# Where the gate products of a batch stand among its token tiles, and how many filler matmuls TensorE gets

## The chip, the cores and the metric

The kernel runs on one core of a Trainium2 chip. The core has TensorE (PE in the profile; its weight loads are PEld), VectorE (DVE), ScalarE (ACT), GpSimd (POOL), and SyncE (SP), which issues most of the transfers. The engines run in parallel. Each takes its own instructions in order and waits on semaphores for the others. TensorE's clock has two levels, 1.2 and 2.4 GHz, and the profile gives the granted clock as a share of the higher one. The metric is the device time of one execution, in microseconds (us), lower being better.

## What is computed

Linear attention without a mask, a norm per head, and then a mixture of eight experts of which each token uses one:

```python
kv = np.einsum('bhsd,bhse->bhde', k, v)          # 8 batches, 8 heads, 576 tokens, 64 wide
out = np.einsum('bhsd,bhde->bhse', q, kv)
out = out / np.sqrt(np.mean(out * out, -1) + 1e-6) * g_norm
x = out                                          # 4608 tokens x 512
logits = x @ w_gate;  e_idx = argmax(logits);  gate_w = softmax(logits)[e_idx]
eom = sigmoid(x @ w_output_gate)
y = gate_w * eom[e_idx] * (relu(x @ w1[e_idx]) @ w2[e_idx])   # 512 -> 1024 -> 512
```

## The kernel before

There are two stages. The first makes all tokens' attention rows and decides each token's expert. It writes the rows to a table `xs` in device memory. The second stage gathers the rows of one expert after another and runs the two large products (`mm1`, `mm2`). The change touches the first stage only.

**The first stage** goes over the 8 batches in `p1_main`. A batch has 576 tokens, which is 4.5 tiles of 128. For batch b, PE does this:

- `kv_part(b)`: 40 products of a head's k with its v, into the PSUM tile `kvps`, over five slices s of the tokens. I call it kv(b). ScalarE copies the result into `augs[b % 3]`, and VectorE copies it into `kvc`.
- `kvT_part`: two transposes of `kvc` into `kvTps`. ScalarE copies them out as `kvT`.
- `m_part(b)`: 8 small products of `kvT` with the gate weights into `mps`. ScalarE copies them into the gate columns of the same `augs` tile. These are the gate products of the title, and I call the step m(b).
- `run_out`: one token tile (`out_tile(g)`, here T0 to T35). It is 8 products of the query with `augs`, into `ops`. The same products give attention rows and gate sums, so a tile of batch b needs m(b). ScalarE empties `ops` with three instructions (`xrow`, `sq`, `gp`).

The tiles that run during batch b are those that batch b-1 completed, so they trail by one batch. In batches 1 to 7 they are T0-3, T4-8, T9-12, T13-17, T18-21, T22-26 and T27-30. T31 to T35 follow after the last batch. `ops` and `mps` share two PSUM buffers (`ps_b`), and `kvps`, `kvTps` and `cps` share two others (`ps_t`).

**Fillers.** `constant` multiplies a tile of ones by itself into a part of PSUM that nobody reads. Its only purpose is to give TensorE something to do. `COLD` holds the numbers: 2 in front of each of the first four slices in the first three batches, 20 more at the start, 2 ahead of `kvT`, 3 ahead of m, and 3 of twice the width behind m in a tile `cps` of their own.

**Routing.** The tiles form four groups: T0-7, T8-15, T16-23 and T24-35. Each has a chain of small VectorE instructions (`route`), which `run_out` moves on by a piece per tile. A chain needs PE twice. `rps` gives positions (after T14, T22 and T27 for the first three groups), and `tblps` fills the table (in front of T17, in front of T26 and behind T30). For each tile of the group `tblps` needs a `la` tile; the first two groups have theirs made on GpSimd, eight in a row, once VectorE has made `rlon`. In VectorE's queue the copy `kvc` of the same batch stands ahead of those pieces. When the third group is placed, its tail (`xtail`) is written to `xs` and the first expert's rows are gathered. From there on the second stage begins.

**Transfers.** SP issues all loads (`ld`: slices `kvm` of keys and values, remainders `rem`, queries `qT`) in the order of `loads`, then the writes of `xrow` and `xtail`, then the weights (`wraw`). PE, ACT, DVE and POOL run in the order of the program text; SP's order is set by a scheduler.

Of the kernel before, what the change touches and what calls it, by code (L numbers as in the profile page):

```python
# [11 lines left out]
F32 = mybir.dt.float32  # L12
# [9 lines left out]
P = 128  # L22
B, H, S, D = 8, 8, 576, 64
# [60 lines left out]


COLD_B = 3
COLD = (2, 20, 2, 3, 3)

ROUND = 1.5 * 2.0 ** 30

# [49 lines left out]
def body(ctx: ExitStack, tc: tile.TileContext, kvm, rem, qT, wg, gn, w1, w2, kc, xs, tab, out):  # L140
    nc = tc.nc
# [27 lines left out]
    ps_t = main.enter_context(tc.tile_pool(name="ps_t", bufs=2, space=psum))  # L169
# [266 lines left out]
    ones = c1.tile([P, P], BF16, name="ones")  # L436
# [45 lines left out]
    def constant(ps, n, start=True):  # L482

        for _ in range(n):
            k = ps.shape[1] // P
            nc.tensor.matmul(ps, ones, ones.unsqueeze(1).to_broadcast([P, k, P]), start=start, stop=start)

    def kv_part(b):

# [3 lines left out]
        for s in range(5):  # L493
            if s < 4 and b < COLD_B:
                constant(ps[:, 256:512], COLD[0] + (COLD[1] if b == 0 and s == 0 else 0), s == 0)
            for p in range(NP):
# [18 lines left out]
    def kvT_part(cp):  # L515

        ps = ps_t.tile([P, 512], F32, name="kvTps", tag="t")
        constant(ps[:, 256:512], COLD[2])
        ps = ps[:, 0:256].rearrange("q (i x) -> q i x", i=2)
        for i in range(2):  # L520
            nc.tensor.transpose(ps[:, i, :], cp[:, i * P:(i + 1) * P], ident)
        t = wk.tile([P, 2, P], F32, name="kvT", bufs=1)
        nc.scalar.copy(t, ps)
        return t

    def m_part(b, kvT):
        a = augs[b % 3]
        ps = ps_b.tile([P, 2, 512], F32, name="mps", tag="big")
        constant(ps[:, 1, 256:512], COLD[3])
        for i in range(2):  # L530
# [61 lines left out]
    def sums():  # L592

        sq, o, gi = squares.pop(0)
        nc.vector.tensor_reduce(out=o, in_=sq, axis=AX.X, op=ALU.add)  # L595
        if gi is not None:
            routing.append(route(gi))
# [212 lines left out]
    def open_rows(late):  # L810
        opened[late] = True
        for w in [w for w in xwrites if (w[0] >= LEAD_TILES) == late]:
            xwrites.remove(w)
            xwrite(*w)

    done_tiles = 0
# [13 lines left out]
    def run_out(limit):  # L830
        nonlocal done_tiles
        if done_tiles < limit:
            out_tile(done_tiles)
            done_tiles += 1
            if len(squares) > 1:
                sums()
            advance()
            load(SPARE)
            if not loads and not opened[0]:
                open_rows(0)  # L840
            if lead_placed and opened[0] and (0, 1, 0) not in raw and (1, 0) not in wgt:
                for c in range(1):
                    wload(0, 1, c)
            for step in HOOKS.get(done_tiles, ""):
                act(step)
# [24 lines left out]
    def p1_main():  # L870
        load(SPARE)
        for b in range(B):
            lim = tiles_ready(b - 1) if b else 0
            cp = kv_part(b)
            load(SPARE)
            run_out(lim)
            kvT = kvT_part(cp)
            run_out(lim)
            run_out(lim)
            m_part(b, kvT)  # L880
            constant(ps_t.tile([P, 512], F32, name="cps", tag="t"), COLD[4])
            while done_tiles < lim:
                run_out(lim)
        while done_tiles < NT:
            run_out(NT)
        for step in TAIL:
            act(step)
        while routing:
            advance()
# [218 lines left out]
    with ExitStack() as p3:  # L1108
# [4 lines left out]
        with tc.For_i(0, nreg) as i:  # L1113
# [19 lines left out]
            for w in (w1, w2):  # L1133
                for c in range(4):
                    t = wo.tile([P, 1024], F32, name=f"ow{len(ws)}")
# [6 lines left out]
            ps = pt.tile([P, 4, P], F32, name="ops")  # L1142
# [68 lines left out]
```

## Time and profile before

| | us |
|---|---|
| median of 3 runs | 588.94 (587.86 to 590.38) |
| the profiled execution's own time | 591.15 |
| its span, first to last instruction | 589.4 |
| PE busy in the span | 562.4 (95%) |

All times below are from the start of the span of the profiled execution. A timeline row has the start, the length, the engine, the source line, the operation, what it writes and reads, and a count; equal neighbours are merged into one row. The length of the last matmul of a row runs over into the next row, so what a step costs on PE is read from start to start. A bracket at the end of a row gives the idle time ahead of it and what ended it.

### The profile page before, as it was taken

What the parts mean: (1) busy time and instruction counts of PE and PEld (TensorE: products, weight loads), DVE (VectorE), ACT (ScalarE), POOL (GpSimd) and SP (SyncE); (2) the same over time, 40 slices, a digit from 0 to 9 for tenths busy, and PEclk for the clock granted to TensorE, in tenths of its full rate; (3) what the DMA queues carried; (4) which work ended last, traced back from release to release, by engine and by line L of the source; (5) the groups of instructions that cost most, each with busy time, mean ns of one, the idle gap of its engine ahead of it and who ended that gap; (6) DMA issues with size and microseconds to landing.
All of it is one profiled execution on the core that took longest, in us unless ns stands there. A gap on an engine that the chain in (4) does not pass through costs nothing.

```text
span 589.4 us, 10666 instructions
## 1 busy us (share of the span) xinstructions
PE 562.4 (95%) x4287; PEld 491.6 (83%) x4287; DVE 258.3 (44%) x562; ACT 223.2 (38%) x411; POOL 145.8 (25%) x150
## 2 busy tenths in 40 slices
PE   7999898869999999999999999999999999999995
PEld 4677777758798998889889987998799889889974
DVE  2136677698325556325531443244334424523410
ACT  1356555643235334323432343235234323532410
POOL 2002330401722511620172027003600540011011
PEclk9899898578999999999999999999999999999998
DMA  8999995681564622342335233524342343200001
GB/s 277 382 408 405 408 374 173 225 295 32 156 254 135 213 78 92 107 159 85 123 95 185 80 108 99 175 72 132 101 153 100 111 165 103 80 36 20 1 19 45
DMA packets 33460, 92.26 MB, mean 157 GB/s; under 512 B 8801, under 2 KB 8929, under 8 KB 33408
## 3 DMA queue, kind: packets, MB, share of 16 engines
q1 hardware_dynamic: 26672, 71.63, 34.5%
q0 software_dynamic: 6304, 19.70, 10.6%
q8 instruction: 35, 0.57, 0.4%
q10 hardware_dynamic: 432, 0.21, 0.1%
q14 instruction: 17, 0.14, 0.1%
HBM read 72.34 MB, written 19.70 MB: 156 GB/s over the span
## 4 chain that ended last, share of the span: by engine, by line
PE 79%; DMA 7%; issue 5%; DVE 4%; POOL 2%; ACT 1%; POOLq 0%; SPq 0%; DVEq 0%
PE hps L322 35%; PE yps L371 33%; PE yps L365 3%; PE tps L284 3%; DMA ld<-qT 2%; PE ops L574 2%; DMA ld<-rem 2%; PE kvps L504 2%; POOL la L752 2%; DMA ld<-kvm 2%; DMA xg<-xs,gidx 1%; DVE ss L595 1%; DMA out<-y,oidx 0%; DVE wlo L222 0%; DVE wlo L229 0%
## 5 line engine op out<-in xcount | busy, mean ns | idle before, releaser
L322 PE MATMUL hps<-xT,whi 128*128 128x256 f32 (+8 forms) x1024 | 192.7, 306 | 5.1 <-DVE hT L338 4.6
L371 PE MATMUL yps<-whi,hT 128*128 128x512 f32 (+3 forms) x592 | 195.0, 398 | 0.0
L322 PEld LDWEIGHTS hps<-xT,whi 128*128 128x128 f32 x1024 | 160.1, 191 | 7.2 <-DVE hT L338 4.2
L371 PEld LDWEIGHTS yps<-whi,hT 128*128 128x128 f32 (+3 forms) x592 | 110.1, 186 | 24.1
L322 PE MATMUL hps<-xT,wlo 128*128 128x304 f32 (+8 forms) x512 | 119.6, 305 | 0.0
L371 PE MATMUL yps<-wlo,hT 128*128 128x512 f32 (+3 forms) x296 | 115.9, 392 | 0.0
L338 DVE SCALAR_TENSOR_TENSOR hT<-hps,hT 128x512 fp32r<-128x512 f32 (+6 forms) x112 | 57.9, 518 | 124.3 <-ACT hT L337 124.3
L337 ACT ACTIVATE hT<-hps 128x512 fp32r<-128x512 f32 (+6 forms) x112 | 51.5, 460 | 144.8 <-PE hps L322 115.0
L322 PEld LDWEIGHTS hps<-xT,wlo 128*128 128x128 f32 x512 | 87.4, 191 | 0.0
L244 POOL DMA_INDIRECT xg<-xs,gidx x42 | 42.7, 1018 | 169.3 <-PE tps L284 91.8
L382 POOL DMA_INDIRECT out<-y,oidx x42 | 44.5, 1059 | 147.9 <-ACT y L381 106.6
L371 PEld LDWEIGHTS yps<-wlo,hT 128*128 128x128 f32 (+3 forms) x296 | 55.1, 186 | 11.2
L222 DVE SCALAR_TENSOR_TENSOR wlo<-wraw,gcol,whi 128x1024 fp32r<-128x1024 f32 x32 | 44.4, 1387 | 40.2 <-ACT whi L219 40.2
L381 ACT ACTIVATE y<-yps,tl 128x512 f32<-128x512 f32 (+3 forms) x37 | 25.5, 688 | 71.4 <-PE yps L371 67.6
L260 POOL TENSOR_TENSOR xg<-xg 128x512 f32<-128x512 f32 (+7 forms) x39 | 41.7, 1072 | 41.0 <-DMA xg<-xs,gidx 33.9
L289 ACT CAST xT<-tps 128x512 fp32r<-128x512 f32 (+9 forms) x45 | 23.2, 518 | 68.7 <-PE tps L284 67.1
L290 DVE TENSOR_TENSOR xT<-tps,xT 128x512 fp32r<-128x512 f32 (+9 forms) x45 | 27.1, 604 | 44.5 <-ACT xT L289 44.0
L229 DVE TENSOR_TENSOR wlo<-wraw,whi 128x1024 fp32r<-128x1024 f32 x32 | 39.2, 1224 | 14.2 <-ACT whi L226 7.1
L574 PE MATMUL ops<-aug,ld 64*128 64x80 f32 (+1 forms) x640 | 41.8, 289 | 0.6 <-issue 0.6
L574 PEld LDWEIGHTS ops<-aug,ld 64*128 64x128 f32 (+1 forms) x640 | 37.3, 194 | 5.8 <-ACT aug L536 3.0
L219 ACT ACTIVATE whi<-wraw,gcol 128x1024 fp32r<-128x1024 f32 x31 | 35.5, 1145 | 0.0
L226 ACT CAST whi<-wraw 128x1024 fp32r<-128x1024 f32 x32 | 33.3, 1041 | 1.7 <-DMA wraw<-w 1.7
(163 smaller groups left out, 400.6 us busy)
## 6 DMA issues: line engine op xcount, KB each, us to landing
wraw<-w SPq DMA_DIRECT2D x64, 512.0 KB, 3.6
ld<-kvm SPq DMA_DIRECT2D x32, 512.0 KB, 10.1
ld<-qT SPq DMA_DIRECT2D x18, 512.0 KB, 10.2
xs<-xrow SPq DMA_DIRECT2D x13, 512.0 KB, 11.6
xs<-xrow SPq DMA_DIRECT2D x2, 1280.0 KB, 15.0
ld<-rem SPq DMA_DIRECT2D x3, 512.0 KB, 10.2
xg<-xs,gidx POOLq DMA_INDIRECT x42, 3.6
out<-y,oidx POOLq DMA_INDIRECT x42, 3.1
```

Source lines behind the costliest of these rows:

```text
L219: he.activation(hi, r, AF.Copy, scale=gcol[:, 0:1])
L222: eng.scalar_tensor_tensor(out=lo, in0=r, scalar=gcol[:, 0:1], in1=hi.bitcast(F32), op0=ALU.mult, op1=ALU.subtract)
L226: he.copy(hi, r)
L229: eng.tensor_tensor(out=lo, in0=r, in1=hi.bitcast(F32), op=ALU.subtract)
L244: gathered = nc.gpsimd.indirect_dma_start(out=x[:M, :], out_offset=None, in_=rows, in_offset=bass.IndirectOffsetOnAxis(ap=gidx[:M, p, t:t ...
L260: eng.tensor_tensor(out=v, in0=v, in1=f, op=ALU.mult)
L322: nc.tensor.matmul(ps[:, j, :n], w[:, o:o + P], x[d][:, j * N:j * N + n], start=(d == 0 and k == 0), stop=(d == 3 and k == 2))
L337: nc.scalar.activation(hh, x, AF.Relu)
L338: nc.vector.scalar_tensor_tensor(out=v(h[:, l:l + n]), in0=x, scalar=0.0, in1=hh.bitcast(F32), op0=ALU.max, op1=ALU.subtract)
L371: nc.tensor.matmul(ps[:M], a, b, start=(f == 0 and k == 0), stop=(f == 7 and k == 2))
L382: i_ = nc.gpsimd.indirect_dma_start(out=out, out_offset=bass.IndirectOffsetOnAxis(ap=oidx[:M, p, t:t + 1], axis=0), in_=y[:M], in_offset=N ...
L574: nc.tensor.matmul(ps[r0:r0 + m, u, p * W:(p + 1) * W], qt[g // 2][r, p, q0:q0 + m], augs[b % 3][r, p, :], start=True, stop=True)
```

## The change

It does four things. In every batch but the last, a second tile goes ahead of `kvT`, and all the remaining tiles go between `kvT` and m, where two stood before (none is left behind m). In the last batch one tile stands there and two come behind m. The fillers are now 1 ahead of `kvT`, 1 ahead of m, and none behind m; those in kv(0) to kv(2) stay. `constant` repeats 64 columns of ones instead of 128, to the same total width. The new helper `cold` is not called.

```diff
-COLD = (2, 20, 2, 3, 3)
+COLD = (2, 20, 1, 1)
...
-            k = ps.shape[1] // P
-            nc.tensor.matmul(ps, ones, ones.unsqueeze(1).to_broadcast([P, k, P]), start=start, stop=start)
+            k = ps.shape[1] // D
+            nc.tensor.matmul(ps, ones, ones[:, 0:D].unsqueeze(1).to_broadcast([P, k, D]), start=start, stop=start)
+
+    def cold():
+        return ps_t.tile([P, 512], F32, name="cps", tag="t")
...
             run_out(lim)
+            if b + 1 < B:
+                run_out(lim)
             kvT = kvT_part(cp)
-            run_out(lim)
-            run_out(lim)
+
+            while done_tiles < (lim if b + 1 < B else lim - 2):
+                run_out(lim)
             m_part(b, kvT)
-            constant(ps_t.tile([P, 512], F32, name="cps", tag="t"), COLD[4])
             while done_tiles < lim:
                 run_out(lim)
```

**PE, batch 3**, a batch of four tiles and no routing on PE. Before, from the two tiles behind `kvT` to kv(4):

```order
L574 MATMUL ops<-aug_117,ld 128x80 x16
L486 LDWEIGHTS ones
L486 MATMUL mps<-ones 128x256
...
L534 MATMUL mps<-gw,kvT 64x16 x8
L486 LDWEIGHTS ones
L486 MATMUL cps<-ones 128x512
...
L574 MATMUL ops<-aug_117,ld 128x80 x8
L504 MATMUL kvps<-ld 64x64 x40
```

The whole of that batch behind kv(3) now:

```order
L577 MATMUL ops<-aug_117,ld 128x80 x16
L486 LDWEIGHTS ones
L486 MATMUL kvTps<-ones 128x256
L524 MATMUL kvTps<-ident,kvc 128x128 x2
L577 MATMUL ops<-aug_117,ld 128x80 x16
L486 LDWEIGHTS ones
L486 MATMUL mps<-ones 128x256
L537 MATMUL mps<-gw,kvT 64x16 x8
L507 MATMUL kvps<-ld 64x64 x40
```

The tile behind m has gone ahead of `kvT` (8 products are one tile), and m now stands directly in front of kv(4).

**PE, batch 4**, where the first group's `tblps` stands. Before, from m(4) to kv(5):

```order
L534 MATMUL mps<-gw,kvT 64x16 x8
L486 LDWEIGHTS ones
L486 MATMUL cps<-ones 128x512
...
L574 MATMUL ops<-aug_115,ld 128x80 x8
L782 LDWEIGHTS la
L782 MATMUL tblps<-rrc,la 128x96
...
L574 MATMUL ops<-aug_115,ld 128x80 x8
L504 MATMUL kvps<-ld 64x64 x40
```

Now, from the two tiles behind `kvT` to kv(5):

```order
L577 MATMUL ops<-aug_115,ld 128x80 x16
L785 LDWEIGHTS la
L785 MATMUL tblps<-rrc,la 128x96
...
L577 MATMUL ops<-aug_115,ld 128x80 x8
L486 LDWEIGHTS ones
L486 MATMUL mps<-ones 128x256
L537 MATMUL mps<-gw,kvT 64x16 x8
L507 MATMUL kvps<-ld 64x64 x40
```

The gate products m(4) and the fillers stood in front of `tblps`; m(4) with its one filler now stands behind it and behind T17. Batch 6 has the same move around T26. VectorE's order does not change at all, and ScalarE's follows PE's.

**SP, at the end of the first stage.** Before:

```order
L804 DMA xs<-xrow 128x2x512 x4
L804 DMA xs<-xtail 128x8x16
L190 TENSOR_LOAD epos
L190 ISA x2
L199 ISA
L199 DMA wraw<-w 128x1024
L804 DMA xs<-xtail 128x8x16
```

Now:

```order
L807 DMA xs<-xrow 128x2x512 x4
L807 DMA xs<-xtail 128x8x16 x2
L190 TENSOR_LOAD epos
L190 ISA x2
L199 ISA
L199 DMA wraw<-w 128x1024
```

The third group's tail has gone in front of the first weight tile's load.

## Rows read from the trace of the kernel before

**Rows 1.** Busy time of each engine from 150 us to the end of the span: length, then busy us of PE, PEld, DVE, ACT and POOL with instruction counts, then granted clock, share of the 16 DMA engines, GB/s.

```profile
150.00:589.40 439.40, 433.07 (x2545) 385.36 (x2544) 166.65 (x286) 151.19 (x240) 117.13 (x112) 1.00 0.33 109
```

**Rows 2.** PE's timeline from the end of kv(2) to kv(4).

```profile
33.70 0.62 PE L504 MATMUL kvps<-ld 64*64 64x64 f32 x14 [0.59 <-DMA ld<-rem]
...
41.73 2.70 PE L504 MATMUL kvps<-ld 128*64 128x64 f32 x80
...
49.03 0.49 PE L486 MATMUL mps<-ones 128*128 128x256 bf16 x3 [0.48 <-ACT gp L582]
49.44 0.42 PE L534 MATMUL mps<-gw,kvT 64*64 64x16 f32 x16
49.80 0.82 PE L486 MATMUL cps<-ones 128*128 128x512 bf16 x3
50.55 1.12 PE L574 MATMUL ops<-aug,ld 64*128 64x80 f32 x16
51.60 2.63 PE L504 MATMUL kvps<-ld 128*64 128x64 f32 x77
```

**Rows 3.** ScalarE's timeline, batches 2 and 3.

```profile
35.01 0.58 ACT L579 COPY xrow<-ops 128x512 f32<-128x512 f32 x1 [0.22 <-PE ops L574]
...
47.13 0.46 ACT L523 COPY kvT<-kvTps 128x256 f32<-128x256 f32 x1
47.60 0.58 ACT L579 COPY xrow<-ops 128x512 f32<-128x512 f32 x1
...
48.74 0.67 ACT L579 COPY xrow<-ops 128x512 f32<-128x512 f32 x1
...
49.93 0.30 ACT L536 COPY aug<-mps 128x64 f32<-128x64 f32 x1
```

**Rows 4.** SP's timeline: when the loads of the keys and values of batches 3, 4 and 7, the first weight tile, and the third group's tail were issued.

```profile
27.28 4.16 SPq L479 DMA_DIRECT2D ld<-kvm  x4
...
34.92 4.23 SPq L479 DMA_DIRECT2D ld<-kvm  x4
...
61.81 4.56 SPq L479 DMA_DIRECT2D ld<-kvm  x4
...
99.26 0.37 SPq L199 DMA_DIRECT2D wraw<-w  x1
101.63 0.36 SPq L804 DMA_DIRECT2D xs<-xtail  x1
```

**Rows 5.** DMA issues on the page: KB each, and the median us from issue to landing.

```profile
wraw<-w SPq DMA_DIRECT2D x64, 512.0 KB, 3.6
ld<-kvm SPq DMA_DIRECT2D x32, 512.0 KB, 10.1
```

**Rows 6.** PE's timeline, end of batch 4: the first group's `tblps`, T17, kv(5), and T18 of batch 5.

```profile
60.85 0.49 PE L782 MATMUL tblps<-rrc,la 128*128 128x96 bf16 x4
...
63.43 0.22 PE L782 MATMUL tblps<-rrc,la 128*128 128x96 bf16 x1 [0.36 <-POOL la L752]
63.58 1.51 PE L574 MATMUL ops<-aug,ld 64*128 64x80 f32 x16
65.01 3.83 PE L504 MATMUL kvps<-ld 128*64 128x64 f32 x80
68.78 1.12 PE L574 MATMUL ops<-aug,ld 64*128 64x80 f32 x16
```

**Rows 7.** GpSimd's timeline: the `la` tiles of the first two groups, and the first gather.

```profile
58.21 5.16 POOL L752 TENSOR_SCALAR la<-ni,rlon 128x128 bf16<-128x128 f32 x8 [9.10 <-DVE rlon L731]
81.56 4.88 POOL L752 TENSOR_SCALAR la<-ni,rlon 128x128 bf16<-128x128 f32 x8 [18.18 <-DVE rlon L731]
...
104.81 1.08 POOL L244 DMA_INDIRECT xg<-xs,gidx  x1 [6.95 <-DVE ss L595]
```

**Rows 8.** Granted clock of three stretches that begin where the clock falls: length, PE busy (instructions), clock, DMA share, GB/s.

```profile
64.20:67.60 3.40, 3.40 (x58) 0.51 1.02 408
...
88.00:91.50 3.50, 3.50 (x70) 0.51 1.07 356
...
101.70:118.70 17.00, 14.91 (x119) 0.50 0.68 223
```

**Rows 9.** PE's timeline: kv(6), the second group's last `tblps`, T26, kv(7); then the third group's `tblps` and T31 to T35.

```profile
75.54 2.63 PE L504 MATMUL kvps<-ld 128*64 128x64 f32 x77
...
86.49 0.22 PE L782 MATMUL tblps<-rrc,la 128*128 128x96 bf16 x1 [0.42 <-POOL la L752]
86.64 1.12 PE L574 MATMUL ops<-aug,ld 64*128 64x80 f32 x16
87.69 4.21 PE L504 MATMUL kvps<-ld 128*64 128x64 f32 x80
...
100.63 0.88 PE L782 MATMUL tblps<-rrc,la 128*128 128x96 bf16 x8 [1.67 <-DVE rrc L769]
101.44 8.27 PE L574 MATMUL ops<-aug,ld 64*64 64x80 f32 x96
```

**Rows 10.** VectorE's timeline: the copy behind kv(7), the third group's tail, and the first use of the first weight tile.

```profile
92.35 0.42 DVE L512 COPY kvc<-kvps 128x256 f32<-128x256 f32 x1 [2.11 <-ACT aug L510]
...
101.43 0.17 DVE L775 TENSOR_TENSOR xtail<-rdn 128x8 f32<-128x8 f32 x1
...
106.30 0.74 DVE L221 TENSOR_SCALAR whi<-wraw,gcol 128x1024 fp32r<-128x1024 f32 x1
```

## The prediction

> **What bounds the kernel now.** I read the busy times by stage first. From 150 us on PE is busy for 433.07 of 439.40 us at the full clock [rows 1]. The change leaves every instruction of that part as it is, so it can only come sooner or later. The question is when the first stage hands over, and that I follow backwards. The first gather starts at 104.81 [rows 7]. It needs the third group's tail, which VectorE writes at 101.43 and SP issues at 101.63 [rows 4, 10]. VectorE's chain for that group runs almost without a break from `kvc` at 92.35, and `kvc` stands there because kv(7) ends on PE at 87.69 + 4.21 = 91.90 [rows 9]. So the number to be found is **the end of kv(7)**; what is behind it keeps its order on VectorE and moves with it.
>
> What sets kv(7)? Not its data: the last of its loads is issued by 61.81 + 4.56 = 66.4 and lands some 10.1 us later [rows 4, 5], at 76.5. It is PE's own chain. Three things make it long: fillers and the wait of m for ScalarE (0.48 us in batch 3) [rows 2]; `tblps`, which waits for the `la` tiles of GpSimd in batches 4 and 6 [rows 6, 7]; and TensorE's clock. The reader is to see that right behind those two waits the granted clock is 0.51, the level of 1.2 GHz, for stretches of 3.4 us [rows 8], and that kv(5) and kv(7), which stand there, take 3.83 and 4.21 us [rows 6, 9] where kv(4) and kv(6) take 2.63 [rows 2, 9].
>
> **The change part by part.** All times are on the profiled execution.
>
> *Batches 0 and 1, and the other form of the fillers:* nothing. A filler keeps its width. kv(2) ends when its remainder has landed, and PE sat idle for 0.59 us for it [rows 2]; these loads depend on no tile. That slack is the cover: if fewer fillers made PE later by more than 0.59 us there, the excess would be paid.
>
> *Batch 2.* kv(2) ends at 33.70 + 0.62 = 34.3, and ScalarE starts on T4 at 35.01 [rows 2, 3]. With the tiles close together ScalarE becomes the pace: a tile costs it 48.74 - 47.60 = 1.14 us back to back, the `kvT` copy 0.47 [rows 3], against 1.05 for a tile on PE (50.55 to 51.60) [rows 2]. m needs the buffer that the fourth tile leaves: 35.01 + 4 x 1.14 + 0.47 = 40.04. One filler (0.41 / 3 = 0.14) and m itself (0.36) [rows 2] make 40.5, where kv(3) now starts at 41.73: 1.2 us sooner. Its last slice lands at about 27.28 + 4.16 + 10.1 = 41.5 [rows 4, 5]; PE comes to it at 40.5 + 1.6 = 42.1, so DMA just allows it.
>
> *Batch 3.* Before, kv(3) to kv(4) is 51.60 - 41.73 = 9.87 us, of which 0.75 are the fillers behind m, 0.41 those ahead of it, and 0.48 m's wait [rows 2]. Now: kv 2.63, the first tile 1.05 and 0.1 until ScalarE has it, three tiles on ScalarE and the `kvT` copy 3 x 1.14 + 0.47 = 3.89, filler and m 0.50; in all 8.2. That saves 1.7. kv(4) starts at 48.7 and ends at 51.3 (before 54.2): 2.9 us sooner. Its last slice (34.92 + 4.23 + 10.1 = 49.2) [rows 4, 5] is needed at 50.3. The m copy on ScalarE (0.30) [rows 3] hides under the 2.63 of the next kv.
>
> *Batch 4.* Here the gain meets a wall. `la` starts 58.21 - 54.2 = 4.0 us after kv(4) ends and takes 5.16 [rows 7]; VectorE's and GpSimd's orders are unchanged, so the last `tblps` goes from 63.43 to 60.5 and no further. What PE no longer does ahead of it, it now waits: it gets there some 5 us behind kv(4) (T13 to T16 and `kvT` at the pace above), at 56.4, and waits 4 us, where before it came at 60.85 and waited under 3. Behind `tblps` stand T17, and now also a filler and m, and kv(5). At the full clock that is 1.05 + 0.50 + 2.63 = 4.2 us; before, without m, it took 68.78 - 63.58 = 5.2 [rows 6] because the clock fell. At 1.2 GHz throughout it is 1.65 for the tile (8.27 us for five tiles at that clock) [rows 8, 9], twice 0.50 for filler and m, and 4.2 for kv(5) (kv(7), nearly all at that clock) [rows 8, 9]: 6.85. The bounds are 4.2 and 6.85. I take 6.85, because the longer and emptier wait is nearest to the third one of this trace, the one in front of T31: PE idle for 1.67 us ahead of `tblps` in one piece, and then a clock of 0.50 for 17.0 us [rows 8, 9]. kv(5) ends at 60.7 + 6.85 = 67.5 (before 68.78): 1.2 us sooner.
>
> Of the clock the Trainium skill ("TensorE: Matmul & The Clock Gate", section "HAM oscillation — how this bites in real kernels") says that waits between short bursts of matmuls put it back, so that each burst starts cold. That speaks against this change, which takes filler work out of waits. The trace agrees as far as it goes: 0.51 behind either `la` wait [rows 8].
>
> *Batch 5* has four tiles and no routing wait: 75.54 - 68.78 = 6.76 [rows 6, 9] becomes 1.15 + 3.89 + 0.50 = 5.54, 1.2 us less. kv(6) ends 2.4 us sooner, at 75.8.
>
> *Batch 6* is batch 4 again. The last `tblps` (86.49) moves with kv(6) to 84.1; T26, filler, m and kv(7) then take 6.85 from 84.25 on and end at 91.1, where it was 91.90 [rows 9]. **0.8 us** of all that was saved is left; with 4.2 in both places it would be 6.2.
>
> *Batch 7 and behind.* `tblps` of the third group waits for VectorE before as after (1.67 us) [rows 9], so a shorter way to it on PE gives nothing. On SP the first weight tile is now issued behind the tail, 101.63 instead of 99.26 in the old times [rows 4]; with the page's median of 3.6 us to land it is there at 101.63 + 0.36 + 3.6 = 105.6, and VectorE wants it at 106.30 [rows 5, 10]: covered, with 0.7 to spare. The far bound is the 10.1 of the loads [rows 5], 5.8 us too late; but those had a full queue ahead of them and this one has not, so I take 3.6 and zero. The tail itself is not delayed.
>
> Sum: -0.8 us on the profiled execution, 591.15 to 590.3 (span 589.4 to 588.6). That execution lies 2.2 us above the median of the runs; I move the median by the same: **588.1 us**.
>
> **The rivals.**
>
> *The clock does not care (faster).* If each of the two low stretches costs what it costs now, 5.2 - 3.7 = 1.5 us, the piece behind `tblps` is 5.7: kv(5) ends 2.4 sooner, kv(6) 3.6, kv(7) at 83.0 + 5.7 = 88.7, 3.2 us sooner, and the kernel takes 585.8. With no low stretch at all it is 6.2: 582.7. For it: the stretches of [rows 8] begin some time after the wait, and both lasted the same 3.4 us. Against it: the waits grow by over a microsecond each.
>
> *The tiles cannot hold the clock (slower).* Tiles in a row, with ScalarE as the pace, replace a mix with full-width fillers. Five tiles alone (T31 to T35) never brought the clock back [rows 8, 9]. If it falls inside a batch without a routing wait (2, 3 or 5) and stays down to the end of the next kv, a batch costs 4.2 + 4 x 1.65 + 0.9 + 1.0 = 12.7 instead of 8.2: 4.5 us. Set against the 0.8, that is 592.6 for one such batch, 597 for two. It decides from the first whole batch on in which the granted clock is at half. Against it: before, the clock is at 1.00 in batches 2, 3 and 5 although PE waits there too; that is with fillers.
> The same page of the Trainium skill, in its section "The HAM clock gate", gives the rule behind this rival (low is the default, activity lifts it) and adds that the same kernel differs from run to run; the three runs before lie within 2.5 us.
>
> *The order moves and nothing is saved (same).* m still stands behind ScalarE, which was its releaser before [rows 2]; if ScalarE's pace in a row is nearer 1.4 than 1.14, batches 2, 3 and 5 save 0.3 to 1 us each, and the pieces behind `tblps` (0.5 of m added to each) take it back: 588.9 to 589.5.
>
> **How the numbers follow.** Forecast 588.1 with 0.50 (its own range 586.5 to 590.5: with 5.7 in place of 6.85 at one of the two waits it is 587.0, with batches 2 and 3 at the longer pace of the third rival 589.5, and the runs before spread by over 1 us to either side), nothing saved 0.14, clock does not care 0.20, clock lost 0.16. Half a per cent is 2.9 us, about what a measurement of this kernel can tell from no change. The first rival lies across that line: I count 0.14 of its 0.20 as faster, and 0.02 of the forecast; the second is slower with all of its 0.16. That gives faster 0.16, same 0.68, slower 0.16. The range leaves out the lower end of the first rival (from 584.8 down) and the second with more than one batch: 584.8 to 592.6.
>
> **What would show it.** In the profile after, kv(4) should start near 48.7, the last `tblps` of batch 4 end near 60.6, kv(6) end near 75.8, kv(7) near 91, and the first gather start near 104. PE's idle time in front of `tblps` should grow, and the granted clock should be at half from T17 to the end of kv(5) and from T26 to the end of kv(7). The forecast is wrong if kv(5) and kv(7) take 2.6 to 3.5 us (first rival), or if the clock is down in 34 to 50 or 68 to 75 us (second). The time from the gather to the end should stay within a microsecond.

## The result, and the profile of the changed kernel

The changed kernel takes 593.27 us (median of 10 runs, 591.77 to 595.65), the kernel before 590.07 us on the same chip (10 runs). The ratio is 1.0056, with an interval of 1.0032 to 1.008: **slower**, by some 3.2 us. The forecast was 588.1, and 592.6 at most. The profiled execution of the changed kernel is 594.78 us (span 592.9), 3.6 us above that of before. I followed the same chain as in the prediction.

Batch 4 first, in the timeline of PE in the changed kernel (start, length, engine, line, operation, count, idle time and its end); it answers to [rows 6]:

```profile
58.28 0.60 PE L785 MATMUL tblps<-rrc,la 128*128 128x96 bf16 x3 [1.48 <-DVE rrc L772]
...
61.55 0.26 PE L785 MATMUL tblps<-rrc,la 128*128 128x96 bf16 x1 [0.32 <-POOL la L755]
61.74 2.00 PE L577 MATMUL ops<-aug,ld 64*128 64x80 f32 x16
63.68 0.40 PE L486 MATMUL mps<-ones 128*128 128x256 bf16 x1
64.00 0.63 PE L537 MATMUL mps<-gw,kvT 64*64 64x16 f32 x16
64.56 4.07 PE L507 MATMUL kvps<-ld 128*64 128x64 f32 x80
68.56 1.68 PE L577 MATMUL ops<-aug,ld 64*128 64x80 f32 x26
```

The last `tblps` is 1.9 us sooner than before, but T17, the filler, m(4) and kv(5) behind it take 6.82 us where it was 5.2, and kv(5) ends at 68.56, 0.2 us sooner. Batch 6, in the same view, answers to [rows 9]:

```profile
85.59 0.26 PE L785 MATMUL tblps<-rrc,la 128*128 128x96 bf16 x1 [0.34 <-POOL la L755]
85.78 2.00 PE L577 MATMUL ops<-aug,ld 64*128 64x80 f32 x16
...
88.59 4.00 PE L507 MATMUL kvps<-ld 128*64 128x64 f32 x80
92.53 1.12 PE L577 MATMUL ops<-aug,ld 64*128 64x80 f32 x16
```

In the kernel before the same row, the tile behind kv(7), is

```profile
91.83 1.12 PE L574 MATMUL ops<-aug,ld 64*128 64x80 f32 x16
```

So kv(7) ends at 92.53 where it ended at 91.83: 0.7 us later instead of 0.8 sooner. The granted clock by stretches (the third figure from the end of each row; answers to [rows 8]):

```profile
34.00:60.80 26.80, 22.71 (x475) 19.67 (x475) 18.33 (x55) 18.56 (x49) 6.82 (x8) 1.00 1.03 408
60.90:67.60 6.70, 6.31 (x92) 5.66 (x93) 1.58 (x6) 1.43 (x4) 0.59 (x2) 0.50 1.03 410
67.70:84.70 17.00, 14.34 (x291) 12.29 (x287) 13.65 (x44) 11.76 (x31) 4.29 (x7) 1.00 1.04 397
84.80:91.50 6.70, 6.17 (x89) 5.52 (x91) 3.75 (x12) 1.43 (x4) 0.73 (x2) 0.50 1.10 349
```

Either of the stretches at half the clock that go with the waits for `la` is now twice as long as before. Then the hand-over, on SP and GpSimd (answers to [rows 4, 7]):

```profile
102.33 0.36 SPq L807 DMA_DIRECT2D xs<-xtail  x1
```

```profile
106.73 1.09 POOL L244 DMA_INDIRECT xg<-xs,gidx  x1 [8.18 <-issue]
108.12 1.04 POOL L244 DMA_INDIRECT xg<-xs,gidx  x1 [0.30 <-issue]
109.46 1.01 POOL L244 DMA_INDIRECT xg<-xs,gidx  x1 [0.31 <-issue]
```

The tail is 0.7 us later, as kv(7) is. But the first gather starts 4.40 us behind the tail's issue, and it was 3.18 (101.63 to 104.81). That is 1.2 us more in a place where the prediction had nothing. The landing events of the trace show where: of the 16 queues that carry the tail, 15 are done 1.96 to 2.12 us behind the issue in either kernel; the last is done at 2.13 before and at 3.44 now. The transfer queues of the changed kernel from 103.6 to 104.8, and of the kernel before over the whole way from tail to gather (101.63 to 104.8):

```profile
q1 hardware_dynamic: 419, 0.04, 25.8%
q8 instruction: 1, 0.02, 4.9%
```

```profile
q1 hardware_dynamic: 1089, 0.20, 29.1%
```

In the changed kernel one packet of 16 KB of the queue named "instruction" runs from 103.76 for 0.93 us, in the middle of the tail. Before, its counterpart ran at 98.84, 2.8 us ahead of the tail. From the first gather to the first `mm1` it takes 11.1 us (before 10.2). The third gather makes that difference: its tile came 5.7 us after its start (109.46 to 115.16), before 4.8 (107.46 to 112.23). On GpSimd, before and now:

```profile
112.23 1.04 POOL L260 TENSOR_TENSOR xg<-xg 128x512 f32<-128x512 f32 x1 [0.95 <-DMA xg<-xs,gidx]
...
115.16 1.04 POOL L260 TENSOR_TENSOR xg<-xg 128x512 f32<-128x512 f32 x1 [2.14 <-DMA xg<-xs,gidx]
```

From the first `mm1` to the end it takes 475.0 us (474.4). So the 3.5 us by which this span is longer are 0.7 at kv(7), 1.2 at the first gather, 0.9 at the third and 0.6 in the second stage.

### The profile page after: what moved, and what is told of

It is laid out like the page before. It is cut to its first block, busy times and chain, and to the rows that moved or that the text cites. A ratio compares the mean times of both kernels' runs of the same rounds, so it can differ in the third digit from the quotient of the medians.

```text
span 592.9 us, 10570 instructions
## 1 busy us (share of the span) xinstructions
PE 558.8 (94%) x4239; PEld 491.8 (83%) x4239; DVE 259.1 (44%) x562; ACT 221.9 (37%) x411; POOL 145.8 (25%) x150
## 4 chain that ended last, share of the span: by engine, by line
PE 79%; DMA 7%; DVE 4%; issue 4%; ACT 3%; POOL 2%; POOLq 0%; SPq 0%; DVEq 0%; ACTq 0%
PE hps L322 35%; PE yps L371 33%; PE yps L365 3%; PE tps L284 3%; PE kvps L507 3%; DMA ld<-qT 2%; DMA ld<-rem 2%; DMA ld<-kvm 2%; POOL la L755 2%; PE ops L577 2%; DMA xg<-xs,gidx 2%; ACT sq L584 1%; ACT xrow L582 1%; DMA out<-y,oidx 0%; ACT gp L585 0%
## 5 line engine op out<-in xcount | busy, mean ns | idle before, releaser
L322 PEld LDWEIGHTS hps<-xT,wlo 128*128 128x128 f32 x512 | 87.2, 191 | 0.0
L577 PE MATMUL ops<-aug,ld 64*128 64x80 f32 (+1 forms) x640 | 43.4, 298 | 2.0 <-ACT rex L722 0.9
L577 PEld LDWEIGHTS ops<-aug,ld 64*128 64x128 f32 (+1 forms) x640 | 38.9, 203 | 5.5 <-ACT gp L585 3.0
## 6 DMA issues: line engine op xcount, KB each, us to landing
ld<-qT SPq DMA_DIRECT2D x18, 512.0 KB, 10.2
```

Of the source, the lines that this page charges most:

```text
L322: nc.tensor.matmul(ps[:, j, :n], w[:, o:o + P], x[d][:, j * N:j * N + n], start=(d == 0 and k == 0), stop=(d == 3 and k == 2))
L577: nc.tensor.matmul(ps[r0:r0 + m, u, p * W:(p + 1) * W], qt[g // 2][r, p, q0:q0 + m], augs[b % 3][r, p, :], start=True, stop=True)
```

## The experiments

Theories: **A**, m and fillers behind the `la` waits, at half the clock, cost what the order saves; in `e1_sp` alone A holds besides that SP's new order (the first weight tile behind the tail) makes the gather late. **B**, SP's new order is harmless, and the gather is late for another reason. **C**, the fillers that were removed had held the clock. **D**, formed after the first four runs: a block of instructions, loaded on one of the queues that carry the tail, holds the last part of the tail up. Readings stand together in the table at the end of this section.

**SP's order put back** (`e1_sp`): the weight tile is loaded ahead of the tail, all else as changed.

```diff
+        if gi == LEAD_GROUP and opened[0]:
+            ahead.append(wload(0, 1, 0))
...
+        if g == GROUPS[LEAD_GROUP][0] and ahead:
+            tc.add_manual_dep(d.ins, ahead[0].ins.name, ...)
```

> The changed kernel with one thing put back: SP issues the first weight tile before the third group's tail, as before the change. Theory A (two causes: the clock behind the la waits makes kv(7) end 0.7 us later, and the swap on SP delays the first gather by another 1.2 us, 4.4 instead of 3.2 us behind the tail's issue): the gather again starts 3.2 us behind the tail, and the ratio to before falls from 1.0056 to between 1.002 and 1.004; kv(5) and kv(7) stay at about 4 us. Theory B (the swap on SP is harmless, and the gather waits longer for another reason, such as GpSimd or the slower PE): the distance stays at 4.4 us and the ratio at 1.005 to 1.006.

Measured: 1.0074 (1.0048 to 1.010). The weight tile goes out at 104.68, ahead of the tail (107.04), and the gather still starts 4.77 us behind the tail. So B holds for the distance, and SP's order is not what makes the gather late; the ratio is above what either theory gave. (The profiled execution took 600.49 us, 6 us above the median of its runs, and its clock was at half from 59.3 to 79.7 us.)

**The order alone, and the fillers alone** (`e2_order`, `e3_fill`).

```diff
 e2_order, against the changed kernel
-COLD = (2, 20, 1, 1)
+COLD = (2, 20, 2, 3, 3)
...
             m_part(b, kvT)
+            constant(cold(), COLD[4])
```

> The change of order alone: the tiles stand ahead of m, but the fillers are 2, 3 and 3 again (the last three now right behind m, so in batches 4 and 6 behind the la wait). Theory A (what hurts is that the work behind the la wait runs at the low clock, and fillers there only lengthen it): ratio 1.006 to 1.010, kv(5) and kv(7) still about 4 us. Theory C (the missing fillers are what costs the clock, in whole batches or in the waits): the clock holds, kv(5) and kv(7) take 2.6 to 3.5 us, ratio 0.997 to 1.002.

```diff
 e3_fill, against the kernel before
-COLD = (2, 20, 2, 3, 3)
+COLD = (2, 20, 1, 1)
...
-            constant(ps_t.tile([P, 512], F32, name="cps", tag="t"), COLD[4])
```

> The change of fillers alone: the order of before, with 1 filler ahead of kvT, 1 ahead of m and none behind it. Theory A: batches 2, 3 and 5 get some 0.8 us shorter each, the la waits of batches 4 and 6 are reached earlier with m already done, and behind them stand only a tile and kv at a low clock; kv(7) ends 0 to 1.5 us sooner than before, ratio 0.997 to 1.001. Theory C (the fillers hold the clock): the clock is at half in batches without a la wait, ratio 1.004 or more.

Measured: the order alone 1.0146 (1.012 to 1.0172), the fillers alone 1.0202 (1.0172 to 1.0233), both together 1.0056. Either half is worse than the whole, and the order alone is worse than A had it (1.010 at most). With the order alone, PE behind the last `tblps` of batch 4:

```profile
63.43 0.26 PE L785 MATMUL tblps<-rrc,la 128*128 128x96 bf16 x1 [0.31 <-POOL la L755]
63.62 2.00 PE L577 MATMUL ops<-aug,ld 64*128 64x80 f32 x16
65.56 0.82 PE L486 MATMUL mps<-ones 128*128 128x256 bf16 x3
66.31 0.63 PE L537 MATMUL mps<-gw,kvT 64*64 64x16 f32 x16
66.87 1.46 PE L486 MATMUL cps<-ones 128*128 128x512 bf16 x3
68.26 3.12 PE L507 MATMUL kvps<-ld 128*64 128x64 f32 x80
```

Here the fillers stand on the path behind the wait: 0.75 + 1.39 us of them, at 1.2 GHz. With the fillers alone removed the clock falls also in batches without a wait for `la` (two of the four stretches at the low clock between 40 and 96 us; kv(6), in the second one, takes 4.5 us):

```profile
41.00:44.20 3.20, 3.20 (x44) 3.06 (x44) 1.74 (x6) 2.69 (x6) 0.00 (x0) 0.50 1.03 405
...
75.10:81.80 6.70, 6.70 (x110) 6.44 (x114) 2.23 (x11) 1.42 (x4) 0.00 (x0) 0.50 1.04 387
```

By these rows A and C hold, each for its half, though not for all of the time: the rows of `e3_fill` are of its fastest execution, 595.32 us where the median is 602.78. The other form of the fillers, 64 columns repeated, did nothing: two of them take 0.39 us in either kernel.

**Fillers inside the waits** (`e4_warm`): 12 of 512 columns in front of the first two groups' table products.

```diff
+WARM = 12
...
+        if gi < 2:
+            constant(cold(), WARM)
         for t in range(n):
```

> The changed kernel with 12 fillers of full width (about 0.25 us each, 3 us in all) right in front of tblps of the first two groups, inside the la wait. Theory A: they cost nothing, as the last la tile sets the end of tblps anyway; the clock is at full behind it, T17 and T26 take 1.05, kv(5) and kv(7) 2.6 us, kv(7) ends near 87.5 us instead of 92.5, and the ratio falls to 0.995 to 0.999 with the swap on SP still in. If low clock behind the waits is not what makes kv(7) late, the ratio stays at 1.005 or rises.

Measured: 1.0038 (1.0019 to 1.0057), not the 0.995 to 0.999 that A gave. kv(7) runs at the full clock and still ends only 0.7 us sooner than before, at 91.11. Its last row on PE:

```profile
90.97 0.21 PE L508 MATMUL kvps<-ld 64*64 64x64 f32 x1 [1.77 <-issue]
```

PE has nothing to wait for that the profile shows. A block of instructions runs from 88.36 to 89.36, and PE goes on 1.6 us after its end. The tail again has a block on it (1.39 us behind its issue) and the gather comes 4.39 us behind the tail. This gave theory D.

**Only the length of PE's stream** (`e5_pad`, on the changed kernel; `e8_padbefore`, on the kernel before, with 78): one-column matmuls, nothing moved.

```diff
+PADS = 70
...
+        if gi == 0:
+            ps = ps_t.tile([P, 512], F32, name="cps", tag="t")
+            for _ in range(PADS):
+                nc.tensor.matmul(ps[:, 0:1], ones, ones[:, 0:1], start=True, stop=True)
```

> The changed kernel with 70 matmuls of one column each in front of the first group's table products, where TensorE waits for GpSimd in any case. They give it no work to speak of, but they make its instruction stream longer, so that the 16 KB blocks of instructions that are loaded over the transfer queues come at other places of the program. Theory D (a block of instructions on one of the 16 queues holds back the last part of the third group's tail, and with it the first gather): no such block runs in the first two microseconds behind the tail's issue, the first gather starts 3.2 us behind it instead of 4.4, and the kernel gains 1 to 1.5 us on the changed one: 1.0030 to 1.0040 of the kernel before. Rival (the gather is late for something else that the new order brings, such as the later tail or the later weight tile): 4.4 us as before, 1.0056. kv(5) and kv(7) should end within 0.4 us of the changed kernel's by either.

> The kernel before with 78 matmuls of one column in front of the first group's table products: nothing but a longer instruction stream, so that the third group's table products stand at the same place of their 16 KB block as in the changed kernel. Theory D: the block that ran at 98.84 us, ahead of the tail, now starts 1 to 2.3 us behind the tail's issue; if it starts by 1.6 us behind it, one queue's part of the tail lands late and the first gather starts 4.3 to 4.8 us behind the issue instead of 3.2, for 1.0015 to 1.0035 of the kernel before. Rival (the new order makes the gather late): 3.2 us and a ratio within 0.999 to 1.001.

Measured: `e5_pad` 1.0055 (1.0023 to 1.0086), `e8_padbefore` 1.0068 (1.0035 to 1.0101). The gather moves as D has it, in both directions. On the changed kernel no block runs on the tail, and the gather starts 3.08 us behind it. On the kernel before, a block now starts 1.14 us behind the tail's issue and takes 1.42; the last queue lands at 4.07, and the gather starts at 107.58, 5.11 us behind (D had 4.3 to 4.8):

```profile
102.47 0.37 SPq L809 DMA_DIRECT2D xs<-xtail  x1
```

```profile
107.58 1.71 POOL L245 DMA_INDIRECT xg<-xs,gidx  x1 [8.88 <-DVE whi L222]
```

The times fit D less well. `e8_padbefore` lost more than the 1.0015 to 1.0035 of D; in its second stage it needs 3.9 us more than the kernel before, as told below. `e5_pad` stayed at the changed kernel's ratio (D had 1.0030 to 1.0040), with a wide interval: PE now ran out of instructions elsewhere, and in that execution the clock fell in kv(4) as well (4.0 us).

```profile
81.86 0.21 PE L720 MATMUL rps<-ohb,triu 128*128 128x72 bf16 x1 [2.00 <-issue]
```

**Fillers in the waits, other places for the blocks** (`e6_warmpad`: 48 of 128 columns in place of 12 of 512) **and fillers in the waits of the kernel before** (`e7_oldwarm`: 6 of 512).

```diff
 e6_warmpad, against the changed kernel
+WARM = 48
...
+        if gi < 2:
+            ps = ps_t.tile([P, 512], F32, name="cps", tag="t")
+            constant(ps[:, 0:P], WARM)
```

> The changed kernel with fillers in both waits for GpSimd's la tiles, as in the run with 12 wide ones, but cut into 48 of 128 columns each: the same columns, and 72 instructions more in each place. Theory D with the full clock behind the waits: kv(5) and kv(7) at 2.6 to 3.6 us as there, the first gather 3.2 us behind the tail's issue, and TensorE not held up for instructions in kv(7) (1.77 us there): the third group's table products start by 98.5 and the kernel takes 0.995 to 0.999 of the kernel before. If the block of instructions falls on the tail again, the gather is 4.4 us behind it and the ratio 1.000 to 1.003. Rival (the late gather belongs to the new order): 4.4 us whatever the blocks do.

> The kernel before with 6 fillers of 512 columns in front of the table products of the first two groups, in their waits for GpSimd; order and other fillers as they were. If the low clock behind those waits is what costs there (1.5 us in kv(5), 1.6 in kv(7)), and gather and second stage follow kv(7): kv(5) and kv(7) take 2.6 to 3.0 us, kv(7) ends 2 to 3 us sooner and the ratio is 0.994 to 0.998. Rival (what TensorE gains there is eaten by the next wait, VectorE's chain of the third group or the loads): kv(7) ends sooner and the third table products do not, ratio 0.999 to 1.002. By theory D it can also lose 1.3 us, if a block of instructions now falls on the tail.

Measured: `e6_warmpad` 0.9953 (0.9926 to 0.998), 588.14 us: faster than both kernels. The gather is 3.09 us behind the tail, and kv(7) ends at 88.03. Set beside `e4_warm` this tells most of what the place of the instruction blocks is worth: the filler columns are the same and only the number of instructions differs, yet 1.0038 became 0.9953 (each against the kernel before on its own chip). Of the 4.4 us in the rows by which the first gather comes sooner (105.29 and 100.91), 1.8 are PE's wait for instructions in kv(7), 1.3 the block on the tail, and 1.2 an earlier end of kv(2), ahead of any difference between the two kernels. `e7_oldwarm` 0.999 (0.9958 to 1.0022): kv(5) and kv(7) take 2.6 us, and the clock (third figure from the end) is 1.00 from 34 to 100.7:

```profile
34.00:100.70 66.70, 61.07 (x1164) 49.85 (x1166) 47.52 (x155) 40.91 (x107) 13.60 (x19) 1.00 0.98 368
```

The tail and the gather are 2.1 us sooner than before, the first `mm1` 1.2 and the end 0.6. One us of it went when the third gather's tile came 5.7 us after its start, in place of 4.8, as in the changed kernel; why, no run here tells. The ratio is the rival's, and its interval holds 1; but the third group's table products do start sooner, at 98.50 instead of 100.63, which the rival excluded.

**m back in front of the waits** (`e9_mfront`; `e10_mwarm` with the fillers of `e6_warmpad`), **the stream of `e6_warmpad` without its work** (`e11_pad48`: one column each), **and the changed kernel again** (`e12_after`).

```diff
 e9_mfront, against the changed kernel
-            while done_tiles < (lim if b + 1 < B else lim - 2):
+            while done_tiles < (lim if b + 1 < B and b not in (4, 6) else lim - 2):
```

> The changed kernel, with m(4) and m(6) and their filler put back in front of the tile that stands ahead of the table products, as before; one tile stands between kvT and m there. Theory A (in those two batches m behind the wait costs on the path, at half the clock): kv(5) and kv(7) start 2.0 to 2.2 us behind the last table product instead of 3.0, the last table products themselves stand in batch 4 where they stood (within 0.2 us), and kv(7) ends 1.6 to 2.0 us sooner than in the changed kernel, at 90.5 to 91. With a block of instructions on the tail again the ratio is 1.002 to 1.003; without one 0.9995 to 1.001. Rival (ScalarE is late for kvT there, and m then holds up the tile and the table products): the last table products are later by what m waits, kv(7) ends within 0.5 us of the changed kernel's, and the ratio stays 1.004 to 1.006.

> The same move of m(4) and m(6), and the 48 fillers of 128 columns in either wait for la as in the fastest run so far. If both gains are independent: kv(5) and kv(7) start 1.2 to 2.1 us behind the last table products, kv(7) ends by 87.2 (87.9 with the fillers alone), and the ratio is 0.990 to 0.994. Rival (what is saved there is lost behind it, as the second stage takes 474 to 478 us from the first mm1 to the end whatever came before): 0.995 to 0.998, as the fillers alone.

> The fastest kernel so far with its 48 fillers in each wait cut to one column: every instruction stands at the same place of the stream as there, but there is no filler work. Against the changed kernel this tells the place of the instruction blocks alone, against the fastest the work of the fillers alone. Theory D: the first gather starts 3.0 to 3.3 us behind the tail's issue, at most 0.6 us of TensorE's waiting is for instructions, and the ratio is 1.0015 to 1.004; kv(5) and kv(7) take 3.8 to 4.5 us at half the clock as in the changed kernel. Rival (the blocks are a detail of one execution, and all of the 2 to 3 us lie in the waits and the clock): 1.005 to 1.0065.

> The changed kernel once more, to be compared on one chip with the three others and for a second trace of it: a ratio of 1.004 to 1.007. By theory D the block of instructions starts 1.1 to 1.6 us behind the tail's issue again and the first gather 4.2 to 4.8 us behind it; by the rival (chance of one execution) the block may stand elsewhere.

Measured: `e9_mfront` 1.0066 (1.0043 to 1.009), `e10_mwarm` 1.0023 (1.0002 to 1.0044), `e11_pad48` 1.0062 (1.0034 to 1.0089), `e12_after` 1.0066 (1.0042 to 1.009). With m ahead, kv(5) and kv(7) start 2.12 us behind the last `tblps` instead of 3.01, as foreseen; in `e10_mwarm` 1.2. The times did not follow: kv(7) was to end by 91 and by 87.2, and ended at 92.18 and 93.20. Batch 6 meets another wall, on ScalarE in `e10_mwarm`:

```profile
81.73 0.59 ACT L583 COPY xrow<-ops 128x512 f32<-128x512 f32 x1 [3.88 <-DMA xs<-xrow]
```

A tile there needs an `xrow` buffer whose earlier content is still to be written to `xs`, and SP starts these writes only behind its loads:

```profile
69.89 10.95 SPq L811 DMA_DIRECT2D xs<-xrow  x8
```

PE stood for 4.17 us, the clock fell, and the 48 fillers took 4.02 us (85.07 to 89.09) instead of 2.69:

```profile
83.15 2.00 PE L578 MATMUL ops<-aug,ld 64*128 64x80 f32 x16 [4.17 <-ACT aug L540]
85.07 4.18 PE L487 MATMUL cps<-ones 128*128 128x128 bf16 x48
```

The copy starts at 80.7 to 82.8 in all eight kernels whose ScalarE waits there, the changed one among them (81.48, a wait of 0.58), however soon PE was. In `e11_pad48` the gather is at 3.08, and yet it is no faster than `e12_after`: its ratio is the rival's and not D's. By its rows the time comes back in the second stage, where it loses 3 us. VectorE, GpSimd and PE there:

```profile
151.49 2.12 DVE L261 TENSOR_TENSOR xg<-xg 128x512 f32<-128x512 f32 x1
```

```profile
152.00 1.05 POOL L261 TENSOR_TENSOR xg<-xg 128x512 f32<-128x512 f32 x1
```

```profile
153.66 1.11 PE L285 MATMUL tps<-ident,xg 128*128 128x128 f32 x4 [2.27 <-DVE tl L281]
```

The same VectorE instruction takes 0.68 us in `e12_after`:

```profile
151.87 0.68 DVE L260 TENSOR_TENSOR xg<-xg 128x512 f32<-128x512 f32 x1
```

PE waits 2.27 us for it, and its clock is at half for 3.4 us behind. The last column of the table falls into three by this: nine executions without that wait need 473.6 to 475.0 us behind the first `mm1`; three with it (2.24 to 2.25 us, the clock held) 475.9 to 476.1; four with it and a fallen clock 477.4 to 478.7.

**The block alone, and the best combination** (`e13_pad56`: on the changed kernel, 56 one-column matmuls in the second group's wait only; `e14_m4warm`: `e6_warmpad` with m ahead in batch 4 only).

```diff
 e13_pad56, against e5_pad          e14_m4warm, against e10_mwarm
-PADS = 70                          -  ... b not in (4, 6) ...
+PADS = 56                          +  ... b != 4 ...
-        if gi == 0:
+        if gi == 1:
```

> The changed kernel with 56 matmuls of one column in front of the second group's table products only, so that batches 0 to 5 are untouched and the third group's table products come 112 instructions later in the stream, about where they stand in the kernel before. Theory D alone, undisturbed: no block of instructions in the first two microseconds behind the tail's issue, the first gather 3.0 to 3.3 us behind it, TensorE never held up for instructions by more than 0.5 us, and a ratio of 1.002 to 1.0045, which is 1.3 us under the changed kernel's on the same chip. Rival (what the gather gains is given back in the second stage as in the run with 48 such matmuls in each wait): gather at 3.1 us, the second stage 3 us longer from the first mm1 to the end, ratio 1.0055 to 1.007.

> The kernel with 48 fillers of 128 columns in either wait, and m moved in front of the table products in batch 4 only; batch 6 as in the changed kernel, because there ScalarE had to wait for the write of an xrow tile (3.88 us) when m stood ahead. If batch 4 keeps the full clock as it did with both moved, kv(5) takes 2.5 instead of 4.0 us, and batch 6 does not wait for m: kv(7) ends at 86 to 87.5 (87.9 without the move, 93.1 with both), ratio 0.992 to 0.9955. Rival (the write of the xrow tile is the wall of batch 6 wherever m stands, so ScalarE waits for it by as much as batch 4 is sooner): kv(7) at 87.5 to 89 or later, ratio 0.995 to 0.9985.

Measured: `e13_pad56` 1.0029 (1.0005 to 1.0052), 591.32 us; `e14_m4warm` 0.9945 (0.9924 to 0.9965), 587.11 us, the lowest of all. In `e13_pad56` the tail is issued at 101.90, and the gather comes 3.08 us later:

```profile
104.98 1.08 POOL L245 DMA_INDIRECT xg<-xs,gidx  x1 [6.86 <-DVE ss L599]
```

PE never waits for instructions, and the second stage takes 474.0. This is D by itself, and its ratio is the one that D gave: 1.6 to 2.2 us less than the changed kernel (1.0056 and 1.0066; the intervals overlap), 1.3 of it in the rows at the gather. Of the three kernels that only keep the block off the tail (`e5_pad`, `e11_pad48`, `e13_pad56`) it is the one that gained; the shift of the gather is shown in all three, its worth in time is not clear of the noise. In `e14_m4warm` ScalarE waits 2.46 us for the `xrow` write in batch 6, yet PE's fillers cover it, the clock is 1.00 from 61.7 to 95.6, and kv(7) ends at 88.76, where the rival had it. Its interval holds the 0.9953 of `e6_warmpad`, so a gain over that kernel is not shown.

Readings from all traces (us; "block" is the start of a 16 KB instruction packet next to the tail, and like "first gather" it is counted from the tail's issue). The ratio is of all runs and the rest of one execution; those of `e1_sp` and `e2_order` took 6.3 and 4.2 us more than the median of their runs, that of `e3_fill` 7.5 us less.

| | ratio | kv(5) from last `tblps` | kv(7) ends | block | first gather | first `mm1` | from there to the end |
|---|---|---|---|---|---|---|---|
| before | 1 | 1.58 | 91.83 | -2.79 | 3.18 | 115.00 | 474.4 |
| changed | 1.0056 | 3.01 | 92.53 | 1.43 | 4.40 | 117.83 | 475.0 |
| e1_sp | 1.0074 | 3.01 | 97.25 | 1.37 | 4.77 | 122.57 | 476.1 |
| e2_order | 1.0146 | 4.83 | 97.72 | 1.25 | 4.34 | 123.28 | 478.7 |
| e3_fill | 1.0202 | 2.12 | 96.24 | 2.32 | 3.19 | 119.62 | 473.9 |
| e4_warm | 1.0038 | 2.29 | 91.11 | 1.39 | 4.39 | 116.17 | 473.7 |
| e5_pad | 1.0055 | 3.01 | 94.87 | -4.23 | 3.08 | 118.26 | 473.6 |
| e6_warmpad | 0.9953 | 1.77 | 88.03 | -2.84 | 3.09 | 111.42 | 477.5 |
| e7_oldwarm | 0.999 | 1.20 | 89.69 | -2.76 | 3.19 | 113.82 | 474.9 |
| e8_padbefore | 1.0068 | 2.80 | 92.67 | 1.14 | 5.11 | 118.68 | 478.3 |
| e9_mfront | 1.0066 | 2.12 | 92.18 | 1.47 | 4.82 | 117.28 | 476.1 |
| e10_mwarm | 1.0023 | 1.20 | 93.20 | -6.27 | 3.18 | 116.59 | 475.9 |
| e11_pad48 | 1.0062 | 3.01 | 93.22 | -5.54 | 3.08 | 116.62 | 477.4 |
| e12_after | 1.0066 | 3.01 | 93.62 | 1.49 | 4.52 | 117.89 | 474.1 |
| e13_pad56 | 1.0029 | 3.01 | 92.10 | -4.06 | 3.08 | 115.49 | 474.0 |
| e14_m4warm | 0.9945 | 1.19 | 88.76 | -3.69 | 3.08 | 112.93 | 474.8 |

In seven executions a block starts 1.1 to 1.5 us behind the tail, and the gather comes after 4.3 to 5.1 us. In the nine others it comes after 3.08 to 3.19.

## Why the prediction was wrong

**The step that failed is *Batch 7 and behind*, which put no change on the way from the tail to the gather ("what is behind it keeps its order on VectorE and moves with it").** On PE, VectorE and SP I looked for what the tail waits for, and priced only the weight tile that SP swaps. That price was nearly right: VectorE waits 0.16 us for the tile (0.67 in `e12_after`), and with the old order of SP nothing was gained (`e1_sp`). What I left out is that with 48 fillers fewer PE's instruction stream is shorter, and its blocks load at other moments, on the same queues as the tail. In rows it costs 1.2 us (3.18 to 4.40); by the ratio of `e13_pad56` it would be 1.6 to 2.2, with intervals that overlap.

**The sum in front of it was mis-sized by 1.5 us**: -0.8 was forecast for the end of kv(7), and +0.7 came; in the second trace of the changed kernel +1.8. The rows of PE that begin the steps, first the last products of kv(2) before, then of the changed kernel the same and the starts of kv(3), kv(4) and kv(6):

```profile
34.15 0.22 PE L504 MATMUL kvps<-ld 64*64 64x64 f32 x2
...
34.54 0.23 PE L507 MATMUL kvps<-ld 64*64 64x64 f32 x2
41.27 2.70 PE L507 MATMUL kvps<-ld 128*64 128x64 f32 x80
49.72 2.63 PE L507 MATMUL kvps<-ld 128*64 128x64 f32 x77
74.38 2.63 PE L507 MATMUL kvps<-ld 128*64 128x64 f32 x77
```

Step by step:

- *Batch 2*: forecast -1.2. The way from the last product of kv(2) to kv(3) fell from 7.57 to 6.72 us, so 0.85; it is 6.71 or 6.72 in all eleven traces with the new order and few fillers. Besides, kv(2) itself ended 0.39 later (34.16 and 34.55); it still waits for its remainder, as before, and its last product starts at 33.7 to 35.8 over all traces, also where the stream up to there is the same. So that part differs by execution.
- *Batch 3*: forecast -1.7, came -1.42 (8.45 to 8.50 from kv(3) to kv(4) in the eleven). The later tiles took ScalarE 1.17 us, and the way from its release to kv(4) was a little longer than the bare lengths that I added, on the side of the third rival.
- *Batch 4*: the mechanism was right. The last `tblps` stands 11.83 us behind the start of kv(4) before and after: the wall at `la`. The piece behind it took 6.82 us (6.85 taken), at half the clock nearly throughout, and kv(5) 4.0. The first rival, that the clock does not care, falls with it.
- *Batch 5*: 5.82 us instead of 5.54. *Batch 6*: 11.21 us from kv(6) to the last `tblps` where I had moved 10.95 along; ScalarE's new wait of 0.58 us for the `xrow` write is in it. That queue on SP I did not look at for batch 6. Behind it 6.75 us (6.85 taken).

**The rival "the tiles cannot hold the clock"** did not decide the changed kernel: its clock was 1.00 in batches 2, 3 and 5 in both traces. It showed in `e5_pad` (kv(4)), in the one execution of `e1_sp`, whose order on PE is that of the changed kernel (all of batch 5), and, with the old order, at two places of `e3_fill`. So it is near; how often it strikes the changed kernel, the traces don't tell. The Trainium skill ("TensorE: Matmul & The Clock Gate", section "HAM oscillation — how this bites in real kernels") would have matmul work stay close together instead of in bursts between waits; the trace agrees, as kv(5) at 3.83 us in the kernel before came down to 2.6 with fillers in the wait (`e7_oldwarm`).

**What is left of the +3.2 us** beside the block is 1.0 to 1.7 us by `e13_pad56` and its ratio. In the rows of the first trace it is 0.7 at kv(7), where the forecast had a gain of 0.8, 0.9 at the third gather and 0.6 behind the first `mm1`. The sign that the time from the gather to the end stays within a microsecond failed by these last two: it grew by 1.6 us. In the second trace the third gather's tile came 4.3 us after its start and the second stage took 474.1, but kv(7) ended 1.1 us later than in the first. So the division differs by execution, by about a microsecond, while the first `mm1` is 2.8 to 2.9 us late in both.

Open are three things. Why the third gather's tile takes 4.3 us in one execution and 5.7 in another is not known. What decides the moment at which a block is loaded was not found: in all seven executions with a block on the tail it came 2.1 to 2.5 us behind the first `tblps` of the third group, in streams of different lengths. And that GpSimd's scaling stretches VectorE's in the second stage is read from rows alone; no run took it away.

## What to carry to other kernels

Filler matmuls belong in front of the instruction that waits, as many as fit in the wait; fillers behind it were paid at the low clock (`e2_order`), and taking fillers away let the clock fall (`e3_fill`). An edit that changes the number of instructions on an engine moves its code loads; compare the landing of each small critical transfer before and after, and if one is late on a single queue, shift the stream by a few idle instructions before the order is blamed. The time need not follow, as the other blocks move too. When a wait is shortened, look for the next user of the buffer: here the writes of `xrow`, queued on SP behind all loads, were the next wall at 81 to 82 us.

## What the runs showed of the hardware

- Instructions are loaded while the kernel runs, in packets of 16,384 bytes (35 in the execution before and in the changed one, 36 with 78 more matmuls in `e8_padbefore`; 0.9 to 1.6 us each, 5 to 11 us apart in the first stage). One of them on one queue made the last sixteenth of a 64 KB write land 1.2 to 1.9 us late.
- PE can run out of instructions: in the first stage it stood for 0.15 to 2.0 us with nothing to wait for that the profile shows (1.77 in `e4_warm`, 2.00 in `e5_pad`, 0.49 already in the kernel before), and each of these waits ended 1.3 to 1.6 us after the end of such a packet.
- One-column matmuls cost 0.025 us each (1.79 us from the first to `tblps` for 70 of them, 1.42 for 56), and did not keep the clock up: it was at half behind them.
- VectorE's scaling of a gathered tile took 2.12 us instead of 0.68 while GpSimd scaled another. The Trainium skill ("SBUF — State Buffer", section "SBUF: two separate sides") says that the two share a port that is locked for a whole instruction. The rows fit that in part: VectorE's instruction ends 0.6 us after GpSimd's, and all seven executions with PE's wait have such a pair. But by that section whichever starts first has the port, and here VectorE started 0.5 us sooner and was the one that was stretched.
